# Projection of a fused convolution and gated FFN: from 128x32 to 64x64 TensorE tiles

## The chip, the cores and the metric

The kernel runs on one core of a Trainium2 chip. The metric is the time of one execution in device microseconds (us); several executions are made and their median is given. Besides the times there is one profiled execution, in which a hardware profiler records every instruction of the engines: TensorE (PE, with its weight loads as PEld), VectorE (DVE), ScalarE (ACT), GpSimd (POOL), SyncE (SP), and the DMA queues that SP, ACT and POOL feed.

## The reference

Two steps follow each other. First a causal lightweight convolution over the sequence: each of 8 heads (24 of 192 channels each) has 7 taps, made positive by a softmax. Then a gated FFN on each of 32768 tokens, from 192 channels to 1536 and back:

```
x: (8, 4096, 192)   weight: (8, 7)
w = softmax(weight, axis=-1)
out = einsum('hk,bskhg->bshg', w, x_unf)      # 7 shifted copies of x
gate = maximum(x @ w_gate, 0.0)               # 192 -> 1536
val = x @ w_val                               # 192 -> 1536
return gate * val @ w_out                     # 1536 -> 192
```

The result is float32, 32768 x 192. The kernel computes its matmuls in float16 with float32 accumulation in PSUM.

## The kernel before

The work is cut into 16 units. A unit holds 1024 consecutive tokens of two batch rows ("streams", `st`), so 2048 tokens, in two windows `w` of 512. The convolved input of a unit, `xc`, has 64 channels of stream 0 on partitions 0 to 63 and the same channels of stream 1 on partitions 64 to 127, in three chunks `c`.

*Gates* (`gate_val`). For each window and each of 12 slices `f` of 128 hidden channels, six matmul pairs are made: three chunks for the gate and three for the value. A pair is two row tiles of 64x128, one per stream, each streaming 512 columns (line 530). ACT applies the relu from PSUM into `gr` (line 539), DVE multiplies it with the value into `hT` (line 540). All PSUM tiles named `ps` (128 x 2 banks x 512) come from one ring of four buffers, in the order of allocation; a slice `f` takes two, so two slices are in flight.

*Projection* (`project_columns`, line 550). After both windows, `hT` (128 hidden channels of one `f` on the partitions) is multiplied with `Wo`. The 192 output channels are cut into three tiles `p` of 64, and these into two banks `b` of 32. A slot consists of four matmuls of 128 rows x 32 columns side by side, one for each pair of window and stream; 12 slots accumulate over `f`. That makes 72 slots, 288 matmuls, per unit. DVE turns each tile by 32x32 blocks into the output buffer `out_s` (`turn_out`, line 564), and `store` sends the unit to DRAM in four DMAs on SP's queue, each from 32 partitions in rows of 192 channels, 768 bytes (line 572). `out_s` has two buffers.

*Convolution of later units.* Units 2 to 15 are convolved by DVE, ACT and POOL beside the matmuls. For unit `u+2`, in unit `u`: POOL copies the loaded `x_e` into `x_p` (line 436), SP transposes it by eight DMA transposes into `x_r` (line 438). During the projection ACT makes the first tap of a part on DVE's account (`lane_first`, line 484) and then 13 products of the other part (line 464), and DVE makes 13 lane steps (lines 495 and 505). `TAPS` and `STEPS` say after which projection tile which products and steps are issued. In the next unit POOL adds the products up (line 473). Each engine works through its instructions in order, and so does SP's queue.

*Start.* Unit 0 and unit 1 are convolved on TensorE with band matrices: `conv(2)` and `conv(3)` make the second part of unit 1 by eight matmuls each (line 353), five ACT copies (line 366) and five DMA transposes (line 385). `conv(3)` stands behind the first projection tile of unit 0. The last unit uses another projection (`project`, line 586) with `Wo` as the moving operand.

What sets the order is the program itself: the schedule is written out by hand, the framework adds the semaphores.

Of the kernel before, what the change touches and what calls it, by code (L numbers as in the profile page):

```python
# [8 lines left out]
FP = mybir.dt.float32  # L9
F16 = mybir.dt.float16  # L10
# [5 lines left out]
def kernel(  # L16
# [12 lines left out]
    nc = tc.nc  # L29

    B, S, D = x.shape
# [4 lines left out]
    NB = B // 2  # L36
    NCH = D // 64
    NBLK = D // 32
    NFF = DFF // 128
    WIN = 512  # L40
    NWIN = S // WIN
    SUB = 112
    STEPS = [4, 5, 4]
    TAPS = [(6, 5, 4), (3, 2), (1, 0)]
    GSUB = 5
    WARM = [2, 3, 1]
    STEPS0 = [1, 0, 2, 3, 4]
# [6 lines left out]
    FLAT = NCH * UNIT  # L54
    LDVE = 1280
# [6 lines left out]
    const = ctx.enter_context(tc.tile_pool(name="const", bufs=1))  # L62
    epool = ctx.enter_context(tc.tile_pool(name="epool", bufs=1))
    rpool = ctx.enter_context(tc.tile_pool(name="rpool", bufs=2))
    apool = ctx.enter_context(tc.tile_pool(name="apool", bufs=1))
# [4 lines left out]
    psum = ctx.enter_context(tc.tile_pool(name="psum", bufs=4, space=bass.MemoryType.PSUM))  # L70
# [5 lines left out]
    def staged(i, j):  # L76
        return stages[i][:, XH * j : XH * (j + 1)]

    def load_x(g, streams=range(2)):


        bp, toks = GROUPS[g]
        xt = staged(g // 3, g % 3).rearrange("p (j s d) -> p j s d", s=2, d=D)
        for st in streams:
            b = bp + NB * st
            last = toks[-1] == S - SUB or toks[-1] - toks[-2] != SUB
            n_full = len(toks) - int(last)
            lo = toks[0] - PAD
            src = bass.AP(
                tensor=x.tensor,  # L90
                offset=x.offset + (b * S + lo) * D,
                ap=[[D, 128], [SUB * D, n_full], [1, D]],
            )
            nc.gpsimd.dma_start(out=xt[:, 0:n_full, st, :], in_=src)
            if last:
                nc.gpsimd.dma_start(
                    out=xt[0 : SUB + PAD, len(toks) - 1, st, :],
                    in_=x[b, toks[-1] - PAD : toks[-1] + SUB, :],
                )
        return xt  # L100
# [61 lines left out]
    with nc.allow_low_precision("one of the terms is not zero"):  # L162
        nc.vector.tensor_reduce(
            out=Z[:, 112 : 112 + HR],
            in_=eye[:].rearrange("p (g i) -> p i g", i=HR),
# [4 lines left out]
        out=mask[:, :, 0],  # L170
        in_=eye[:].rearrange("p (g i) -> p g i", i=HR),
# [17 lines left out]
    for half in range(2):  # L189
        nc.tensor.matmul(  # L190
            out=raised[half][:, 0, 0 : SUB * H // 2],
            lhsT=zeros[:, 0:128],
            rhs=zeros[:, 0 : SUB * H // 2],
            start=True,
            stop=False,
# [2 lines left out]

    Wg = const.tile([128, NCH, DFF], F16)
    Wv = const.tile([128, NCH, DFF], F16)  # L200
    Wo = const.tile([128, NFF, D], F16)
    CUTS = [0, 128, 256, 512, 896, DFF]
    HALVES = [0, 128, 256, 512, 896, 1280, DFF]

# [16 lines left out]
    for s in range(5):  # L221
# [8 lines left out]
        out=mx[:], in_=spread[:, 0, 0:KW], axis=mybir.AxisListType.X, op=ALU.max, negate=True  # L230
# [8 lines left out]
        out=prod[:],  # L239
# [11 lines left out]
        out=blocks[:],  # L251
# [11 lines left out]
    for half, copy in enumerate((nc.vector.tensor_copy, nc.scalar.copy)):  # L263
        for j in range(128 // HR):
# [3 lines left out]
                out=raised[half][:, 0, 0 : SUB * H // 2].rearrange("p (h t) -> p h t", t=SUB)[  # L268
                    :, :, s0 + lo : s0 + hi
                ],  # L270
                lhsT=Z[:, 112 - HR * j : 240 - HR * j],
                rhs=blocks[:, H // 2 * half : H // 2 * (half + 1), lo:hi],
                start=False,
                stop=(j == 128 // HR - 1),
# [3 lines left out]
            out=bands[half][:].rearrange("p h t -> p (h t)"), in_=raised[half][:, 0, 0 : SUB * H // 2]  # L278
# [7 lines left out]
    for c in range(NCH):  # L286
        r0 = 0
        while r0 < 64:
# [3 lines left out]
            for st in range(2):  # L292
                nc.sync.dma_start(
                    out=tap[64 * st + r0 : 64 * st + r1, c, :],
# [158 lines left out]
    def shifted(u, c, k, t, n):  # L453
        o = HALO - KW + 1 + k + t
        return xrs[u][:, c, o : o + n]
# [4 lines left out]
    def product(u, k):  # L460
        prods[u, k] = apool.tile([128, FLAT - LDVE], FP, name=f"prod{k}")
        for at, n, c, t in pieces(LDVE, FLAT):
            if k or t == 0:
                nc.scalar.activation(  # L464
                    out=prods[u, k][:, at - LDVE : at - LDVE + n],
                    in_=shifted(u, c, k, t, n),
                    func=ACTF.Copy,
                    scale=tap[:, c, k : k + 1],
                )
# [70 lines left out]
            nc.vector.tensor_tensor(out=h[:, f], in0=gr[:], in1=pss[1][:], op=ALU.mult)  # L540
        return h

    def project_columns(hs, p):


        ps = psum.tile([128, 2, 512], FP, name="ps")
        for b in range(2):
            for f in range(NFF):
                for s in range(4):
                    nc.tensor.matmul(  # L550
                        out=ps[32 * s : 32 * s + 32, b, :],
                        lhsT=Wo[:, f, 64 * p + 32 * b : 64 * p + 32 * b + 32],
                        rhs=hs[s // 2][:, f, s % 2, :],
                        start=(f == 0),
                        stop=(f == NFF - 1),
                        tile_position=(0, 32 * s),
                        skip_group_check=True,
                    )
        return ps

    def turn_out(ps, o, p):


        nc.vector.transpose(  # L564
            out=o[:, :, 64 * p : 64 * p + 64].rearrange("p t (b c) -> p b t c", b=2),
            in_=ps[:].rearrange("p b (t c) -> p b t c", c=32),
        )

    def store(o, bp, w0):
        for s in range(4):  # L570
            row0 = (bp + NB * (s % 2)) * S + WIN * (w0 + s // 2)
            nc.sync.dma_start(
                out=out[row0 : row0 + WIN, :].rearrange("(t p) d -> p t d", p=32),
                in_=o[32 * s : 32 * s + 32],
            )

    def project(bp, w, h, st, final, o):


        parts = [range(4)] if not final else [range(2), range(2, 3), range(3, 4)]  # L580
        row0 = (bp + NB * st) * S + WIN * w
        for n, qs in enumerate(parts):
            ps = psum.tile([128, 2, 512], FP, name="ps")
            for i, q in enumerate(qs):
                for f in range(NFF):
                    nc.tensor.matmul(  # L586
                        out=ps[:, i // 2, D * (i % 2) : D * (i % 2) + D],
                        lhsT=h[:, f, st, 128 * q : 128 * (q + 1)],
                        rhs=Wo[:, f, :],
                        start=(f == 0),  # L590
                        stop=(f == NFF - 1),
                    )
            os_ = o[:, qs[0] : qs[0] + len(qs), :].rearrange("p (a b) d -> p a (b d)", a=(len(qs) + 1) // 2)
            k = len(qs)
            a, m = (k + 1) // 2, min(k, 2) * D
            copy = nc.vector.tensor_copy if n == 1 else nc.scalar.copy
            copy(out=os_, in_=ps[:, 0:a, 0:m])  # L597
            (nc.scalar if n == 2 else nc.sync).dma_start(
                out=out[row0 + 128 * qs[0] : row0 + 128 * (qs[0] + k), :].rearrange(
                    "(q p) d -> p q d", p=128  # L600
                ),
                in_=o[:, qs[0] : qs[0] + k, :],
            )
# [12 lines left out]
    both_halves(nc.vector.tensor_copy, 1, Wv)  # L616
    lane_load(2)
    xts[2] = load_x(2)
    nc.gpsimd.dma_start(out=Wo[:], in_=moe_w_out.rearrange("(c p) d -> p c d", p=128))
    for u in range(NUNIT):  # L620
        lane = 1 <= u < NUNIT - 1
        if lane:
            add(u + 1, 1)
        if u == 1:
            lane_load(3)
            add(2, 2)
            add(2, 3)
        if u + 2 < NUNIT:
            lane_turn(u + 2)
        if u == 0:  # L630
            xts[3] = load_x(3)
        if 0 < u < NUNIT - 3:
            lane_load(u + 3)
        if lane:
            for k in range(4 if u == 1 else 2, KW - 1):
                add(u + 1, k)
        hs = [gate_val(u, w) for w in range(2)]
        if lane:
            add(u + 1, KW - 1)
        if u == 0:  # L640
            xc[1] = xcpool.tile([128, NCH, UNIT], F16, name="xc")
            conv(2)
        del xc[u]
        bp, w0 = u * UNIT // S, u * UNIT % S // WIN
        lane = None
        if u + 2 < NUNIT:
            lane_first(u + 2)
            lane = lane_rest(u + 2)
        o = opool.tile([128, UNIT // 64, D], FP, name="out_s")
        if u == NUNIT - 1:  # L650
            for i in range(4):
                project(bp, w0 + i // 2, hs[i // 2], i % 2, i == 3, o[:, 4 * i : 4 * i + 4, :])
            continue
        for p in range(3):
            ps = project_columns(hs, p)
            if lane:
                for k in TAPS[p]:
                    product(u + 2, k)
                for _ in range(STEPS[p]):
                    next(lane)  # L660
            turn_out(ps, o, p)
            if u == 0 and p == 0:
                conv(3)
        store(o, bp, w0)


# [28 lines left out]
```

## Time and profile before

| what | value |
|---|---|
| median of 3 runs | 768.77 us (767.99 to 769.97) |
| profiled execution | 768.63 us |
| its span | 766.9 us |
| TensorE busy | 761.4 us, 99% |
| DVE busy | 670.9 us, 87% |
| ACT busy | 598.6 us, 78% |
| POOL busy | 422.9 us, 55% |
| granted TensorE clock | 0.999 of full |
| chain by line | 530: 64.9%, 550: 30.6%, 586: 2.1% |

The profiled execution takes 1.7 us more than its span, which runs from the first to the last instruction. In a group of instructions, "busy, mean ns" is the total busy time and the duration of one; matmul durations overlap, so their pace is read from starts and from the chain, not from the mean. "idle before" is the time that the engine stood still ahead of these instructions, with what ended it. The chain of work that ended last is followed back from the end: what stands on it sets the time.

### The profile page before, as it was taken

To read this page: it belongs to the slowest core of one execution; us is meant where nothing else is said; L and a number is where in the kernel's file an instruction comes from. 1 tells how busy PE (TensorE), PEld (TensorE's weight loads), DVE (VectorE), ACT (ScalarE), POOL (GpSimd) and SP (SyncE) were. 2 spreads that over 40 slices of the span, in tenths; PEclk is the share of its full clock that TensorE was granted. 3 is DMA by queue.
4 is the path that set the end of the run, shared out by engine and by line. 5 is a ranking of instruction groups with operands and counts; after the bars stand their busy time and mean duration, and the time that the engine had idled before them with its cause. 6 is when DMAs were issued, how large, how long until landed. Compare 5 with 4: busy or idle time off the path is not lost.

```text
span 766.9 us, 21548 instructions
## 1 busy us (share of the span) xinstructions
PE 761.4 (99%) x9402; PEld 378.6 (49%) x9402; DVE 670.9 (87%) x630; ACT 598.6 (78%) x622; POOL 422.9 (55%) x190
## 2 busy tenths in 40 slices
PE   8999999999999999999999999999999999999998
PEld 5554444444444444444444444444444444444448
DVE  6888999989899998989989899898998989896690
ACT  6798887978778787787978879788797877874471
POOL 9407749095591946829277391864909558191000
PEclk9999999999999999999999999999999999999999
DMA  9927829092390905609065190832909142040402
GB/s 143 152 51 130 92 58 111 3 136 31 78 90 3 150 17 93 74 15 152 2 107 61 36 131 3 127 40 60 107 3 138 29 82 45 2 84 2 83 2 83
DMA packets 123214, 53.79 MB, mean 70 GB/s; under 512 B 87648, under 2 KB 123120, under 8 KB 123120
## 3 DMA queue, kind: packets, MB, share of 16 engines
q1 hardware_dynamic: 86192, 38.06, 31.5%
q0 software_dynamic: 36768, 14.26, 18.3%
q8 instruction: 73, 1.20, 0.7%
q14 instruction: 21, 0.17, 0.1%
q10 hardware_dynamic: 160, 0.10, 0.0%
HBM read 29.40 MB, written 25.17 MB: 71 GB/s over the span
## 4 chain that ended last, share of the span: by engine, by line
PE 99%; ACT 0%; POOL 0%; DVE 0%; issue 0%; POOLq 0%
PE ps L530 65%; PE ps L550 31%; PE ps L586 2%; PE ps L330 0%; PE ps L353 0%; PE ps L180 0%; DVE hT L540 0%; ACT gr L539 0%; PE ps L267 0%; PE ps L190 0%; ACT xc L341 0%; PE ps L186 0%; POOL prod L160 0%; POOL rows L144 0%; ACT out_s L597 0%
## 5 line engine op out<-in xcount | busy, mean ns | idle before, releaser
L539 ACT ACTIVATE gr<-ps 128x1024 f16<-128x1024 f32 x384 | 393.2, 1024 | 146.4 <-PE ps L530 146.1
L540 DVE TENSOR_TENSOR hT<-gr,ps 128x1024 f16<-128x1024 f16 x384 | 468.9, 1221 | 38.5 <-ACT gr L539 12.0
L473 POOL TENSOR_TENSOR prod<-prod,prod 128x1792 f32<-128x1792 f32 x70 | 278.6, 3980 | 257.6 <-DVE prod L505 212.4
L530 PE MATMUL ps<-xc,Wg 64*128 64x512 f16 x2304 | 312.1, 376 | 0.6 <-ACT xc L341 0.6
L530 PE MATMUL ps<-xc,Wv 64*128 64x512 f16 x2304 | 311.9, 376 | 0.2 <-DVE hT L540 0.2
L550 PE MATMUL ps<-hT,Wo 128*32 128x512 f16 x4320 | 236.0, 379 | 0.0
L530 PEld LDWEIGHTS <-Wv 64*128 64x128 f16 x2304 | 129.9, 94 | 119.0 <-issue 0.5
L530 PEld LDWEIGHTS <-Wg 64*128 64x128 f16 x2304 | 111.2, 94 | 138.8 <-issue 6.9
L550 PEld LDWEIGHTS <-Wo 128*32 128x32 f16 x4320 | 114.1, 97 | 120.3 <-issue 6.3
L464 ACT ACTIVATE prod<-x_r,tap 128x1024 f32<-128x1024 f16 (+1 forms) x182 | 172.9, 1043 | 0.1
L495 DVE SCALAR_TENSOR_TENSOR acc<-x_r,tap,acc 128x1024 f32<-128x1024 f16 (+1 forms) x140 | 114.2, 873 | 2.4 <-ACT acc L484 2.4
L564 DVE STREAM_TRANSPOSE out_s<-ps 128x1024 f32<-128x1024 f32 x45 | 56.1, 1247 | 33.2 <-PE ps L550 33.1
L473 POOL TENSOR_TENSOR xc<-prod,prod 128x1792 f16<-128x1792 f32 x14 | 55.7, 3976 | 1.1
L436 POOL COPY x_p<-x_e 128x1536 f16<-128x1536 f16 x28 | 40.3, 1468 | 2.1 <-DMA x_e<-in_x_dram 2.1
L399 POOL DMA_DIRECT2D x_e<-in_x_dram x28 | 25.1, 900 | 4.2 <-POOL x_p L436 4.2
L495 DVE SCALAR_TENSOR_TENSOR xc<-x_r,tap,acc 128x1024 f16<-128x1024 f16 (+1 forms) x28 | 23.4, 878 | 0.0
L484 ACT ACTIVATE acc<-x_r,tap 128x1024 f32<-128x1024 f16 (+1 forms) x28 | 21.6, 823 | 0.5 <-DMA x_r<-x_p 0.5
L586 PE MATMUL ps<-Wo,hT 128*128 128x192 f16 x192 | 16.0, 246 | 0.0
L586 PEld LDWEIGHTS <-hT 128*128 128x128 f16 x192 | 15.8, 98 | 0.4 <-issue 0.4
L597 ACT COPY out_s<-ps 128x768 f32<-128x768 f32 (+2 forms) x5 | 3.2, 639 | 12.7 <-PE ps L586 12.7
L597 DVE COPY out_s<-ps 128x192 f32<-128x192 f32 x1 | 0.4, 358 | 13.3 <-PE ps L586 13.3
L505 DVE TENSOR_SCALAR prod<-x_r,tap 128x768 f32<-128x768 f16 x14 | 8.6, 612 | 0.0
(55 smaller groups left out, 62.8 us busy)
## 6 DMA issues: line engine op xcount, KB each, us to landing
out_dram<-out_s SPq DMA_DIRECT2D x63, 384.0 KB
x_e<-in_x_dram POOLq DMA_DIRECT2D x28, 384.0 KB, 10.2
x_r<-x_p SPq DMA_TRANSPOSE x112
out_s<-in_x_dram POOLq DMA_DIRECT2D x4, 240.0 KB, 6.8
prod<-in_x_dram SPq DMA_DIRECT2D x3, 192.0 KB
Wo<-in_moe_w_out_dram POOLq DMA_DIRECT2D x1, 576.0 KB, 10.5
out_s<-in_x_dram POOLq DMA_DIRECT2D x2, 192.0 KB, 4.7
Wg<-in_moe_w_gate_dram POOLq DMA_DIRECT2D x1, 240.0 KB, 6.1
```

What stands on the lines that cost most here:

```text
L399: nc.gpsimd.dma_start(out=xe[:, :, st, :, :].rearrange("p j c r -> p j (c r)"), in_=bass.AP(tensor=x.tensor, offset=x.offset + row * D, ap ...
L436: nc.gpsimd.tensor_copy(out=xp[:, :, :, st, :], in_=xe[:, :, st, :, :])
L464: nc.scalar.activation(out=prods[u, k][:, at - LDVE : at - LDVE + n], in_=shifted(u, c, k, t, n), func=ACTF.Copy, scale=tap[:, c, k : k + 1],)
L473: nc.gpsimd.tensor_tensor(out=p0[:] if k < KW - 1 else flat(u)[:, LDVE:FLAT], in0=p0[:], in1=prods.pop((u, k))[:], op=ALU.add,)
L484: nc.scalar.activation(out=accs[u][:, at : at + n], in_=shifted(u, c, 0, t, n), func=ACTF.Copy, scale=tap[:, c, 0:1],)
L495: nc.vector.scalar_tensor_tensor(out=(flat(u) if k == KW - 1 else acc)[:, at : at + n], in0=shifted(u, c, k, t, n), scalar=tap[:, c, k : k ...
L530: nc.tensor.matmul(out=pss[i][:, st, :], lhsT=W[64 * st : 64 * st + 64, c, 128 * f : 128 * (f + 1)], rhs=xcb[64 * st : 64 * st + 64, c, WI ...
L539: nc.scalar.activation(out=gr[:], in_=pss[0][:], func=ACTF.Relu)
L540: nc.vector.tensor_tensor(out=h[:, f], in0=gr[:], in1=pss[1][:], op=ALU.mult)
L550: nc.tensor.matmul(out=ps[32 * s : 32 * s + 32, b, :], lhsT=Wo[:, f, 64 * p + 32 * b : 64 * p + 32 * b + 32], rhs=hs[s // 2][:, f, s % 2, ...
L564: nc.vector.transpose(out=o[:, :, 64 * p : 64 * p + 64].rearrange("p t (b c) -> p b t c", b=2), in_=ps[:].rearrange("p b (t c) -> p b t c" ...
L586: nc.tensor.matmul(out=ps[:, i // 2, D * (i % 2) : D * (i % 2) + D], lhsT=h[:, f, st, 128 * q : 128 * (q + 1)], rhs=Wo[:, f, :], start=(f ...
```

## The change

Each projection slot now consists of four 64x64 tiles: two halves `r` of the 128 hidden channels by two streams `st`, and all 64 output channels of a tile `p` at once. A half `r` of the rows writes one bank (window `b`), the other half the other bank; so in one turn each bank gets only half of the sum. A second turn of 12 slots swaps the halves and completes both. Matmuls, slots and streamed columns per unit are the same in number.

Between the two turns of a tile ACT copies one column of each bank out (`between_turns`), and the second turn's matmuls wait for it. The six turns of the three tiles are interleaved: (0,0), (1,0), (0,1), (2,0), (1,1), (2,1), as (tile, turn). Products are issued after first turns and lane steps before the transpose after second turns, with new `STEPS` and `TAPS`; `conv(3)` stands behind turn (2,0).

`Wo` is laid out anew, so that a tile `p` holds channels 32p to 32p+31 and 96+32p to 96+32p+31. It is loaded into the buffer `prod0` and regrouped by two POOL copies in unit 0. The partitions of `out_s` now stand for stream and half row, so the store has eight DMAs, each of rows of 96 channels, 384 bytes.

```diff
-    STEPS = [4, 5, 4]
-    TAPS = [(6, 5, 4), (3, 2), (1, 0)]
+    STEPS = [6, 5, 2]
+    TAPS = [(6, 5), (4, 3), (2, 1, 0)]
...
-    def project_columns(hs, p):
-        ps = psum.tile([128, 2, 512], FP, name="ps")
-        for b in range(2):
-            for f in range(NFF):
-                for s in range(4):
+    def project_turn(hs, p, ps, turn):
+        for f in range(NFF):
+            for r in range(2):
+                b = (r + turn) % 2
+                for st in range(2):
                     nc.tensor.matmul(
-                        out=ps[32 * s : 32 * s + 32, b, :],
-                        lhsT=Wo[:, f, 64 * p + 32 * b : 64 * p + 32 * b + 32],
-                        rhs=hs[s // 2][:, f, s % 2, :],
-                        start=(f == 0),
-                        stop=(f == NFF - 1),
-                        tile_position=(0, 32 * s),
+                        out=ps[64 * st : 64 * st + 64, b, :],
+                        lhsT=Wo[64 * r : 64 * r + 64, f, p, :],
+                        rhs=hs[b][64 * r : 64 * r + 64, f, st, :],
+                        start=(turn == 0 and f == 0),
+                        stop=(turn == 1 and f == NFF - 1),
+                        tile_position=(64 * r, 64 * st),
                         skip_group_check=True,
                     )
-        return ps
+
+    def between_turns(ps):
+        nc.scalar.copy(out=turned_by[:], in_=ps[:, :, 0])
...
-            out=o[:, :, 64 * p : 64 * p + 64].rearrange("p t (b c) -> p b t c", b=2),
+            out=o[:].rearrange("p t (b d) -> p b t d", b=2)[:, :, :, 32 * p : 32 * p + 32],
...
-        for s in range(4):
-            row0 = (bp + NB * (s % 2)) * S + WIN * (w0 + s // 2)
-            nc.sync.dma_start(
-                out=out[row0 : row0 + WIN, :].rearrange("(t p) d -> p t d", p=32),
-                in_=o[32 * s : 32 * s + 32],
-            )
+        for q in range(4):
+            row0 = (bp + NB * (q // 2)) * S + WIN * w0
+            for b in range(2):
+                nc.sync.dma_start(
+                    out=out[
+                        row0 + WIN * b : row0 + WIN * (b + 1), D // 2 * (q % 2) : D // 2 * (q % 2 + 1)
+                    ].rearrange("(t p) d -> p t d", p=32),
+                    in_=o[32 * q : 32 * q + 32, :, D // 2 * b : D // 2 * (b + 1)],
+                )
...
-    nc.gpsimd.dma_start(out=Wo[:], in_=moe_w_out.rearrange("(c p) d -> p c d", p=128))
+    loaded = apool.tile([128, FLAT - LDVE], FP, name="prod0")
+    plain = loaded[:].bitcast(F16)[:, 0 : NFF * D]
+    nc.gpsimd.dma_start(
+        out=plain.rearrange("p (c d) -> p c d", d=D), in_=moe_w_out.rearrange("(c p) d -> p c d", p=128)
+    )
...
+            wide = plain.rearrange("k (f a p d) -> k f a p d", a=2, p=3, d=32)
+            for a in range(2):
+                nc.gpsimd.tensor_copy(out=Wo[:, :, :, 32 * a : 32 * a + 32], in_=wide[:, :, a, :, :])
...
-        for p in range(3):
-            ps = project_columns(hs, p)
-            if lane:
-                for k in TAPS[p]:
-                    product(u + 2, k)
-                for _ in range(STEPS[p]):
-                    next(lane)
-            turn_out(ps, o, p)
-            if u == 0 and p == 0:
-                conv(3)
+        tiles = [None] * 3
+        for p, turn in ((0, 0), (1, 0), (0, 1), (2, 0), (1, 1), (2, 1)):
+            if turn == 0:
+                tiles[p] = psum.tile([128, 2, 512], FP, name="ps")
+            project_turn(hs, p, tiles[p], turn)
+            if turn == 0:
+                between_turns(tiles[p])
+                if lane:
+                    for k in TAPS[p]:
+                        product(u + 2, k)
+                if u == 0 and p == 2:
+                    conv(3)
+                continue
+            if lane:
+                for _ in range(STEPS[p]):
+                    next(lane)
+            turn_out(tiles[p], o, p)
         store(o, bp, w0)
```

More of the change, by code (lines that the diff above doesn't have):

```diff
@@ L200 @@
     Wv = const.tile([128, NCH, DFF], F16)
-    Wo = const.tile([128, NFF, D], F16)
+    Wo = const.tile([128, NFF, 3, 64], F16)
     CUTS = [0, 128, 256, 512, 896, DFF]
@@ L541, in gate_val @@
         return h
-    def project_columns(hs, p):
-        ps = psum.tile([128, 2, 512], FP, name="ps")
-        for b in range(2):
-            for f in range(NFF):
-                for s in range(4):
-                    nc.tensor.matmul(
-                        out=ps[32 * s : 32 * s + 32, b, :],
-                        lhsT=Wo[:, f, 64 * p + 32 * b : 64 * p + 32 * b + 32],
-                        rhs=hs[s // 2][:, f, s % 2, :],
-                        start=(f == 0),
-                        stop=(f == NFF - 1),
-                        tile_position=(0, 32 * s),
+    def project_turn(hs, p, ps, turn):
[3 more added lines that the diff above has]
+                for st in range(2):
+                    nc.tensor.matmul(
+                        out=ps[64 * st : 64 * st + 64, b, :],
[4 more added lines that the diff above has]
+                        tile_position=(64 * r, 64 * st),
                         skip_group_check=True,
                     )
-        return ps
+    turned_by = const.tile([128, 2], FP)
+    def between_turns(ps):
+        nc.scalar.copy(out=turned_by[:], in_=ps[:, :, 0])
     def turn_out(ps, o, p):
         nc.vector.transpose(
-            out=o[:, :, 64 * p : 64 * p + 64].rearrange("p t (b c) -> p b t c", b=2),
+            out=o[:].rearrange("p t (b d) -> p b t d", b=2)[:, :, :, 32 * p : 32 * p + 32],
             in_=ps[:].rearrange("p b (t c) -> p b t c", c=32),
@@ L588, in project @@
                         lhsT=h[:, f, st, 128 * q : 128 * (q + 1)],
-                        rhs=Wo[:, f, :],
+                        rhs=Wo[:, f, :, :].rearrange("k p (a d) -> k a p d", a=2),
                         start=(f == 0),
```

## The prediction

> **What bounds the kernel now.** I read busy shares first, then the chain in order of time, then the end of one projection engine by engine, then the DMA queue of SyncE. The page and the chain of work that ended last:
>
> ```profile
> PE 761.4 (99%) x9402; PEld 378.6 (49%) x9402; DVE 670.9 (87%) x630; ACT 598.6 (78%) x622; POOL 422.9 (55%) x190
> L550 PE MATMUL ps<-hT,Wo 128*32 128x512 f16 x4320 | 236.0, 379 | 0.0
> L484 ACT ACTIVATE acc<-x_r,tap 128x1024 f32<-128x1024 f16 (+1 forms) x28 | 21.6, 823 | 0.5 <-DMA x_r<-x_p 0.5
> ...
> 107.42 31.19 PE ps L530 x288
> 138.60 15.65 PE ps L550 x288
> 154.26 31.19 PE ps L530 x288
> ```
>
> TensorE never stops: each unit costs 31.19 + 15.65 = 46.84 us of it. 31.19 us over 144 row-tiled pairs is 216.6 ns a pair; 15.65 us over 72 groups of four is 217.4 ns, and inside the projection a group starts 215.7 ns after the one before. Both stream 512 columns per slot, so only the array's pace, its switches between tile shapes, and new waits can move the time. Now one projection (it starts at 138.53) on ACT, DVE, POOL and PE, in the timeline:
>
> ```profile
> 137.79 0.81 PE L530 MATMUL ps<-xc,Wv 64*128 64x512 f16 x6
> 138.53 0.83 PE L550 MATMUL ps<-hT,Wo 128*32 128x512 f16 x12
> ...
> 138.92 1.54 ACT L484 ACTIVATE acc<-x_r,tap 128x1024 f32<-128x1024 f16 x2
> 140.36 12.33 ACT L464 ACTIVATE prod<-x_r,tap 128x768 f32<-128x768 f16 x13
> 155.05 1.02 ACT L539 ACTIVATE gr<-ps 128x1024 f16<-128x1024 f32 x1 [2.36 <-PE ps L530]
> ...
> 140.19 3.27 DVE L495 SCALAR_TENSOR_TENSOR acc<-x_r,tap,acc 128x1024 f32<-128x1024 f16 x4
> 143.95 1.25 DVE L564 STREAM_TRANSPOSE out_s<-ps 128x1024 f32<-128x1024 f32 x1 [0.49 <-PE ps L550]
> 154.31 1.25 DVE L564 STREAM_TRANSPOSE out_s<-ps 128x1024 f32<-128x1024 f32 x1 [1.11 <-PE ps L550]
> ...
> 153.35 3.99 POOL L473 TENSOR_TENSOR prod<-prod,prod 128x1792 f32<-128x1792 f32 x1 [17.44 <-DVE prod L505]
> ```
>
> ACT has 2.36 us to spare per projection; DVE waits for TensorE before its last transpose. And SyncE's queue, then DMA share and rate in two windows (last two columns):
>
> ```profile
> 45.51 18.39 SPq L385 DMA_TRANSPOSE xc<-out_s  x10
> 64.00 4.96 SPq L572 DMA_DIRECT2D out_dram<-out_s  x4
> 80.10 11.22 SPq L438 DMA_TRANSPOSE x_r<-x_p  x8
> 92.65 1.55 ACT L484 ACTIVATE acc<-x_r,tap 128x1024 f32<-128x1024 f16 x2 [0.47 <-DMA x_r<-x_p]
> ...
> 155.59 4.55 SPq L572 DMA_DIRECT2D out_dram<-out_s  x4
> 160.34 15.38 SPq L438 DMA_TRANSPOSE x_r<-x_p  x8
> ...
> 156.50:160.50 4.00, 4.00 (x42) 1.94 (x38) 3.78 (x4) 3.19 (x4) 3.82 (x4) 1.00 0.98 183
> 757.00:759.00 2.00, 2.00 (x27) 2.00 (x25) 0.00 (x0) 0.00 (x0) 0.00 (x0) 1.00 0.62 197
> ```
>
> Stores and the x_r transposes share one queue in order. In steady state x_r has landed some 9 us before ACT's L484 asks for it (transposes over at 175.7, L484 at 185.8). In unit 1 it is already late: ACT waited 0.47 us at 92.65. In the windows a store of 768-byte packets from 32 partitions runs at 183 GB/s / (0.98 x 16) = 11.7 GB/s an engine, 66 ns a packet; the last stores, from 128 partitions, at 197 / (0.62 x 16) = 19.9, 39 ns.
>
> **The change, part by part.**
>
> *Matmuls.* 288 per unit before and after, in 72 slots of four 512-column streams. A gain in pace is excluded: every row streams about 2.37 columns a ns. The nearest rows are the groups of four (215.7 ns) and the pairs whose two halves are row tiles, as the new ones are (216.6 ns). I take the second: 0.9 ns x 72 x 15 = **+1.0 us** (ends 0 and 1.0). Weight loads double to 64 columns. A run of 40 conv matmuls (L330), half of them with 32-column loads, takes 0.57 us of the chain, so such a load costs at most 14 ns; four of 64 columns, at most 114 ns, lie under a 216 ns slot as long as they overlap it.
>
> *Switches of tile shape.* L530 to L550 costs 0.09 us over the usual step (137.79 to 138.53 is 0.74, six matmuls being 0.65), back 0.10. Whether 64x128 to 64x64 is a switch no row shows. I keep it: 0; without it, 30 x 0.095 = -2.8 us. [...]
>
> *Fences on ACT.* Each first turn is followed by a 128x2 copy on ACT (rows for tiny operations: 0.20 and 0.27 us; I take 0.27), and the second turn of that tile waits for it. Turns last 12 x 215.7 = 2.59 us; an end reaches another engine 0.24 us later (143.95 - 138.53 - 5.18). Counted from the projection's start: L484 ends at 1.93; fence 0 waits for 2.83, done 3.10, needed at 5.18; four products of 0.948 us (12.33 / 13) to 6.89; fence 1 done 7.16, needed 10.35; four more; fence 2 done 11.2, needed 12.94; five products to 16.0. The next gate's first relu (L539) is due at 155.05 - 138.53 = 16.52. So TensorE waits nowhere: 0, covered by ACT's 2.36 us idle, of which 0.5 us is left. Queued behind each fence are the products and then that relu; once the 0.5 us is gone, TensorE stops for the rest, since the third gate group needs the first one's buffers.
>
> *DVE.* Six lane steps from 1.66 end at 6.6; transpose 0 waits for turn 3 (7.77 + 0.24) and ends at 9.2; five steps to 13.5, transpose 1 to 14.7, two short steps to 15.7, transpose 2 at 15.78, as before (154.31 - 138.53). 0.
>
> *GpSimd.* Its first add starts when the last products end, at 16.0 instead of 14.8: x_p 1.2 us later, behind the store in SP's queue anyway; 0. The two Wo copies of unit 0 (128x1152; L436 copies 1536 in 1.47 us) fall into an idle stretch from 32 to 61 us, 9 us ahead of the projection that needs them: 0.
>
> *Half rows, steady state.* Eight stores, 4096 packets of 384 bytes, in place of four with 2048. By bytes a packet costs half of 64 ns, 32; by packets 64; x_e's 384-byte load packets take 51 (DMA records). I take 45. The store then flows 256 x 45 = 11.5 us an engine instead of 16, at most 16.4: x_r lands 3 to 8 us later, inside its 9. 0; the cover ends near 77 ns a packet.
>
> *The start: conv(3) and unit 1.* conv(3) moves behind turn (2,0), its five ACT moves (2.0 us) behind all products, to 60.1 to 62.1. Its PSUM pair now comes after the three tiles, so the second gate group of unit 1 (61.15) needs the buffer of transpose 2, free at 61.9: **+0.75 us**. Its DMA transposes go from 62.1; the fifth waits for the fourth's landing, as before (4.5 us), so SP reaches the store at about 71.7 instead of 64.0. Eight issues, two free and six at the flow's 1.44 us, plus some 2 us against the x_e load: SP is free at 83.3 instead of 80.1. Eight transposes of x_r (11.2 us) and 1.3 us to be seen: 95.8 instead of 92.65. L484 then ends at 97.35, fence 0 at 97.6, just when TensorE needs it (92.44 + 5.18), but ACT's products end at 110.6 against a relu due at 108.96: **+1.6 us**. Ends: at 32 ns SP is free at 80 and this is 0; at 64 ns x_r comes at 99.3, fence 0 holds TensorE 3.5 us and the relu is 1.6 us late: 5.1.
>
> Sum: 1.0 + 0.75 + 1.6 = 3.35 on the profiled 768.63 (span 766.9 + 1.7): 772.0, with the median 0.14 above it 772.1. 0.3% (2.3 us) is about what can be told from no change.
>
> **Rivals.**
>
> A. The shape change is none, because the row halves stay: 0.095 us x 30 gone. 768.77 + 3.35 - 2.8 = 769.3, and with the two upper terms at their low ends (0 and 0) 768.77 + 0.75 - 2.8 = 766.7: not slower. It decides (under the 2.3 us) once a switch falls by 0.035 us, and gives a gain only with the upper terms low. For it: the change keeps two row halves throughout. Against: nothing in the trace switches columns alone at full clock.
>
> B. Half rows hold x_r back in every unit. Past 77 ns a packet each ns is 0.256 us a unit on ACT's products and the next relu: at 84 ns 1.8 us x 12 units + 8 at the start, 798. For it: 66 against 39 ns shows that these stores already suffer from their source. Against: bytes per packet halve. [...]
>
> C. Quarters don't overlap as halves do: loads of 64 columns laid bare cost up to 114 x 1080 = 123 us (892). Against: 97 ns loads are hidden at L550 and L530 alike.
>
> D. ACT falls behind in every unit: fences that cost 0.5 us each rather than 0.27, or a late wake-up, use 0.7 us and more of its 0.5: with 1 us in all too much, 14 units give 786. For it: only 0.5 us is left; against: the 0.27 us row.
>
> **How the numbers follow.** Forecast 0.45, A 0.25, B 0.10, C 0.07, D 0.13. The forecast's own range is 769.5 to 776 (terms 0.75 to 6.9); A reaches down to 766.5; D and most of B lie under 792; left out are C, the worst of B and a little below. Faster: half of A, 0.12. Within 0.3%: the other half and the forecast's low part, 0.30. Slower: the rest, 0.58.
>
> **What would show it.** Steady projections on the chain of 15.65 to 15.75 us, gates 31.19; more says C, less than 15.6 says A. A gap of TensorE before unit 1's first gates and another about 108 to 112 us; none elsewhere. ACT's wait for x_r once in unit 1, not later; if in each, B. ACT's relu waiting 0.5 us instead of 2.36 after each projection; if it waits for nothing and TensorE does, D. Store packets near 45 ns. I am wrong if TensorE idles over 0.1 us in a steady unit.

## The result and the profile after

The changed kernel takes 769.9 us in the median of 12 executions, the one before 768.42 us in the same row: a ratio of 1.0019, 95% interval 1.0011 to 1.0026. Two more rows, told below, give 1.0008 (0.9999 to 1.0017) and 1.0010 (1.0001 to 1.0019). So its median is 0.1 to 0.2% higher in all three rows, 0.6 to 1.5 us where 3.35 were forecast, and in one row the interval still touches no change. It also spreads more: 768.9 to 771.93 us.

Two lines of the page of the changed kernel, busy shares and the new projection's matmuls:

```profile
PE 761.2 (99%) x9402; PEld 392.1 (51%) x9402; DVE 670.4 (87%) x630; ACT 603.8 (79%) x667; POOL 424.8 (55%) x192
...
L550 PE MATMUL ps<-hT,Wo 64*64 64x512 f16 x4320 | 236.2, 376 | 0.0
```

TensorE is as full as before. The chain in order of time (start, duration, what) says where the little that was lost lies:

```profile
60.51 31.32 PE ps L530 x288
91.84 15.66 PE ps L550 x288
107.50 31.30 PE ps L530 x288
138.80 15.66 PE ps L550 x288
154.46 31.19 PE ps L530 x288
185.65 15.66 PE ps L550 x288
```

From unit 3 on a unit takes 31.19 + 15.66 = 46.85 us, against 46.84. Units 1 and 2 have gates of 31.32 and 31.30. From there on the units of the two kernels agree to 0.01 us. ACT at unit 1's projection, in the changed kernel's timeline:

```profile
94.62 1.55 ACT L484 ACTIVATE acc<-x_r,tap 128x1024 f32<-128x1024 f16 x2 [2.38 <-DMA x_r<-x_p]
96.08 0.13 ACT L563 COPY turned_by<-ps 128x2 f32<-128x2 f32 x1
96.12 3.84 ACT L464 ACTIVATE prod<-x_r,tap 128x768 f32<-128x768 f16 x4
...
103.69 4.88 ACT L464 ACTIVATE prod<-x_r,tap 128x768 f32<-128x768 f16 x5
108.47 2.14 ACT L539 ACTIVATE gr<-ps 128x1024 f16<-128x1024 f32 x2
```

The wait for x_r has grown from 0.47 to 2.38 us, and at 108.47 two relus stand back to back: ACT came late to unit 2. DVE came late too, since its lane steps wait for L484. Its last transpose of unit 1, and the group of unit 2 that needs the buffer of this transpose:

```profile
108.15 1.25 DVE L568 STREAM_TRANSPOSE out_s<-ps 128x1024 f32<-128x1024 f32 x1
109.45 0.82 PE L530 MATMUL ps<-xc,Wv 64*128 64x512 f16 x6
```

The transpose ends at 109.40 and the group starts at 109.45, 0.06 us later than its turn. A steady unit's ACT, for comparison:

```profile
141.56 0.16 ACT L563 COPY turned_by<-ps 128x2 f32<-128x2 f32 x1 [0.92 <-PE ps L550]
...
155.26 1.02 ACT L539 ACTIVATE gr<-ps 128x1024 f16<-128x1024 f32 x1 [0.93 <-PE ps L530]
```

Here ACT still has 0.93 us to spare before the first relu. SP's queue in the changed kernel, up to unit 2:

```profile
45.42 27.41 SPq L385 DMA_TRANSPOSE xc<-out_s  x10
72.93 7.31 SPq L577 DMA_DIRECT2D out_dram<-out_s  x8
80.33 13.01 SPq L438 DMA_TRANSPOSE x_r<-x_p  x8
```

conv(3)'s transposes hold SP until 72.8 us, the first store comes after them, and the x_r transposes for unit 3 after that, until 93.3 instead of 91.3. They start only 0.2 us later than before (80.33 against 80.10). The rest is their run, 13.0 us instead of 11.2: in the DMA records the store's packets move until 87.8 us, beside them, where before they had ended at 77.7.

### The profile page after: what moved, and what is told of

Read it like the earlier page. It is cut to its first block, busy times and chain, and to the rows that moved or that the text cites. A ratio compares the mean times of both kernels' runs of the same rounds, so it can differ in the third digit from the quotient of the medians.

```text
span 767.0 us, 21736 instructions
## 1 busy us (share of the span) xinstructions
PE 761.2 (99%) x9402; PEld 392.1 (51%) x9402; DVE 670.4 (87%) x630; ACT 603.8 (79%) x667; POOL 424.8 (55%) x192
## 4 chain that ended last, share of the span: by engine, by line
PE 99%; ACT 0%; DMA 0%; DVE 0%; issue 0%
PE ps L530 65%; PE ps L550 31%; PE ps L593 2%; PE ps L330 0%; PE ps L353 0%; DMA w<-in_weight_dram 0%; PE ps L180 0%; DVE hT L540 0%; PE ps L267 0%; ACT gr L539 0%; PE ps L190 0%; ACT xc L341 0%; PE ps L186 0%; ACT out_s L604 0%
## 5 line engine op out<-in xcount | busy, mean ns | idle before, releaser
L540 DVE TENSOR_TENSOR hT<-gr,ps 128x1024 f16<-128x1024 f16 x384 | 468.7, 1221 | 36.9 <-ACT gr L539 10.2
L530 PE MATMUL ps<-xc,Wg 64*128 64x512 f16 x2304 | 312.8, 376 | 0.6 <-ACT xc L341 0.6
L530 PE MATMUL ps<-xc,Wv 64*128 64x512 f16 x2304 | 312.7, 376 | 0.2 <-DVE hT L540 0.2
L550 PE MATMUL ps<-hT,Wo 64*64 64x512 f16 x4320 | 236.2, 376 | 0.0
L530 PEld LDWEIGHTS <-Wv 64*128 64x128 f16 x2304 | 131.0, 94 | 118.3 <-issue 0.6
L530 PEld LDWEIGHTS <-Wg 64*128 64x128 f16 x2304 | 113.5, 94 | 136.4 <-issue 6.7
L550 PEld LDWEIGHTS <-Wo 64*64 64x64 f16 x4320 | 124.9, 107 | 109.9 <-issue 6.3
L464 ACT ACTIVATE prod<-x_r,tap 128x1024 f32<-128x1024 f16 (+1 forms) x182 | 175.0, 1043 | 0.0
L563 ACT COPY turned_by<-ps 128x2 f32<-128x2 f32 x45 | 7.0, 155 | 22.6 <-PE ps L550 20.8
L484 ACT ACTIVATE acc<-x_r,tap 128x1024 f32<-128x1024 f16 (+1 forms) x28 | 21.6, 821 | 2.4 <-DMA x_r<-x_p 2.4
```

The source lines that it names most:

```text
L464: nc.scalar.activation(out=prods[u, k][:, at - LDVE : at - LDVE + n], in_=shifted(u, c, k, t, n), func=ACTF.Copy, scale=tap[:, c, k : k + 1],)
L484: nc.scalar.activation(out=accs[u][:, at : at + n], in_=shifted(u, c, 0, t, n), func=ACTF.Copy, scale=tap[:, c, 0:1],)
L530: nc.tensor.matmul(out=pss[i][:, st, :], lhsT=W[64 * st : 64 * st + 64, c, 128 * f : 128 * (f + 1)], rhs=xcb[64 * st : 64 * st + 64, c, WI ...
L550: nc.tensor.matmul(out=ps[64 * st : 64 * st + 64, b, :], lhsT=Wo[64 * r : 64 * r + 64, f, p, :], rhs=hs[b][64 * r : 64 * r + 64, f, st, :] ...
```

## The experiments

Two theories stood against each other. S, the start: the whole loss lies in units 0 to 2, by way of conv(3)'s late place, the late first store and a late x_r, and it varies with the landing of that x_r. W, the whole run: the new projection or its stores cost something in every unit. A third, H, joined later: long executions are long in the head, before the first projection.

**The first store behind the transposes.** The changed kernel; only the order on SP differs, once:

```diff
             lane_turn(u + 2)
+        if u == 1:
+            store(*unit0)
...
-        store(o, bp, w0)
+        if u == 0:
+            unit0 = o, bp, w0
+        else:
+            store(o, bp, w0)
```

> The changed kernel with the store of unit 0 issued after the eight transposes of x_r for unit 3, so that SP is free for them as soon as x_p is copied (80.3 us). Theory S: ACT's wait for x_r in unit 1 falls from 2.4 us to 0.5 us or less, the gaps of 0.05 us at 109 and 110 us go, the one at 61 us (0.12) stays; median 768.7 to 769.1 (ratio 1.000 to 1.001) and a spread as narrow as that of before. Theory W: the median stays at 769.5 to 770.5 although the wait is gone.

Beside it ran the changed kernel itself:

> The changed kernel once more, in one row with the others, and a second trace of it. In its first trace it lost 0.27 us against the profiled execution of before (0.13 us ahead of unit 1's second gate group, 0.12 us early in unit 2), while its median was 1.5 us up with a spread of 3 us. Theory S (start): the rest of the loss is also at the start, where x_r of unit 3 lands at a different time in each execution: this trace, if it is a longer one, shows steady units of 46.85 us all the same and longer gaps in units 1 and 2. Theory W (whole run): steady units differ, each a little longer than 46.85 us. Time by both: 769.5 to 770.5, ratio about 1.002.

Measured: the changed kernel 769.05 us, 1.0008 (0.9999 to 1.0017); with the first store behind, 768.75 us, 0.9998 (0.9989 to 1.0007). The timeline of ACT in the second:

```profile
92.25 1.53 ACT L484 ACTIVATE acc<-x_r,tap 128x1024 f32<-128x1024 f16 x2
...
108.41 1.02 ACT L539 ACTIVATE gr<-ps 128x1024 f16<-128x1024 f32 x1 [0.93 <-PE ps L530]
```

The wait for x_r is gone and unit 2 begins like every other unit. Unit 1 keeps its gap at 61 us and has another of 0.11 us at 76 us, where the last of conv(3)'s late transposes lands (76.09) just after TensorE wanted it; in the first trace it had landed at 73.93. The steady units are 46.85 us too, so what W would name is still in it, and the kernel is as fast as before within the interval. The trace of the changed kernel in this row shows something that S did not hold: an execution of 769.73 us whose ACT wait was only 1.5 us and whose unit 2 lost nothing. Its delay lies at 22 us:

```profile
20.75 0.23 PE L330 MATMUL ps<-band,out_s 118*32 118x112 f16 x2
22.15 0.63 PE L330 MATMUL ps<-band,out_s 118*32 118x112 f16 x38 [1.17 <-DMA out_s<-in_x_dram]
```

A load of x for conv(1) arrived late. The change does not touch that load. That made theory H, and the pair was run again.

> The changed kernel a third time, beside the next one on the same chip, for the spread: in the run before, 6 of 11 executions of it were above 769.0 us, none of 11 with the first store behind the transposes, 5 of 33 of the kernel before. Theory S: again about half above 769, the longer executions because x_r of unit 3 lands later. Theory H (head): the long executions differ in the first 25 us, where loads of x arrive late (the second trace had a wait of 1.2 us for one at 22 us); then the two kernels of this pair have the same share of long executions.

> The changed kernel with the first store behind the x_r transposes, a second time. Theory S: at most 1 or 2 of 11 above 769.0, median 768.5 to 768.9. Theory H: as many long executions as the changed kernel beside it.

Measured: the changed kernel 769.23 us, 1.0010 (1.0001 to 1.0019), 8 of 11 executions above 769.0; with the first store behind 768.68 us, 1.0002 (0.9994 to 1.0011), 2 of 11. Over both rows it is 14 of 22 against 2 of 22, and 7 of 60 for the kernel before. H alone would give the pair equal shares: it explains single executions, not the difference.

**conv(3) ahead.** In the changed kernel conv(3) follows conv(2), before the projection:

```diff
             conv(2)
+            conv(3)
...
-                if u == 0 and p == 2:
-                    conv(3)
```

> The changed kernel with conv(3) right behind conv(2), ahead of the first projection. Theory S: its ACT moves end about 47.5 us instead of 61, the first store starts when transpose 2 is done (62.0), x_r for unit 3 is as early as before (ACT waits 0.5 us or less), and the gaps at 61 and 109 us go; a new gap of about 0.7 us opens at 44.7 us, where the first projection tile needs a buffer of conv(2) until its moves end at 45.4. Median 768.9 to 769.5, narrow spread. Theory W: 769.5 to 770.5 plus that gap.

Measured: 768.71 us, 1.0005 (0.9996 to 1.0013). SP's queue in the timeline:

```profile
45.31 16.56 SPq L385 DMA_TRANSPOSE xc<-out_s  x10
62.03 7.31 SPq L577 DMA_DIRECT2D out_dram<-out_s  x8
79.28 11.41 SPq L438 DMA_TRANSPOSE x_r<-x_p  x8
```

The first store starts at 62.03 and the transposes at 79.28, no later than before (64.00 and 80.10). TensorE at conv(3)'s new place:

```profile
44.39 0.57 PE L353 MATMUL ps<-out_s,band 118*112 118x240 f16 x4 [0.32 <-DVE hT L540]
```

ACT no longer waits for x_r and the gaps of units 1 and 2 are gone, as S said. The new gap came where I had not put it: inside conv(3), which waits for DVE's last multiply, not before the projection tile. It is 0.48 us from start to start (582 ns where 102 is the step).

**Half rows alone.** The kernel before, each of its four stores cut in two:

```diff
-                out=out[row0 : row0 + WIN, :].rearrange("(t p) d -> p t d", p=32),
-                in_=o[32 * s : 32 * s + 32],
+                out=out[row0 : row0 + WIN, D // 2 * b : D // 2 * (b + 1)].rearrange("(t p) d -> p t d", p=32),
+                in_=o[32 * s : 32 * s + 32, :, D // 2 * b : D // 2 * (b + 1)],
```

> The kernel before with nothing but its stores cut into half rows (eight DMAs of 384-byte packets per unit in place of four of 768). Theory S: unit 0's store is done on SP at about 71.3 us, ahead of the x_p copy (80.1), so nothing moves: ratio 0.9995 to 1.0005. Theory W, in the form that half rows cost something in every unit: ratio 1.001 to 1.002. Packets of 32 ns in both.

Measured: 768.38 us, 0.9999 (0.9990 to 1.0007). Its SP queue ends the first store at 61.70 + 7.46 = 69.2 us, ahead of the transposes at 77.97. Half rows cost nothing in themselves.

**conv(3) late, alone.** The kernel before, with its old projection and full rows:

```diff
-            if u == 0 and p == 0:
+            if u == 0 and p == 2:
                 conv(3)
```

> The kernel before with nothing but conv(3) moved behind the third projection tile (full rows, 128x32 tiles, no fences). Theory S (the start makes the loss): a gap of 0.1 to 1 us ahead of unit 1's second gate group, the first store reaches SP about 72 us instead of 64, x_r of unit 3 is seen about 2 us late; without fences TensorE does not wait for ACT's late L484, so beyond the gap nothing: ratio 1.0002 to 1.0015. Theory W (loss in every unit of the new projection): ratio 0.9995 to 1.0005, since no unit has the new projection.

Measured: 769.37 us, 1.0011 (1.0003 to 1.0020): a loss like that of the changed kernel, without any of its new matmuls, fences or half rows. TensorE in its timeline:

```profile
62.85 0.82 PE L530 MATMUL ps<-xc,Wg 64*128 64x512 f16 x6
64.11 0.82 PE L530 MATMUL ps<-xc,Wv 64*128 64x512 f16 x6 [0.43 <-DVE hT L540]
```

And ACT, one projection later:

```profile
95.37 1.55 ACT L484 ACTIVATE acc<-x_r,tap 128x1024 f32<-128x1024 f16 x2 [2.82 <-DMA x_r<-x_p]
...
109.06 1.91 ACT L539 ACTIVATE gr<-ps 128x1024 f16<-128x1024 f32 x2
```

The last transpose of DVE there, and the group of unit 2 behind it:

```profile
108.90 1.25 DVE L564 STREAM_TRANSPOSE out_s<-ps 128x1024 f32<-128x1024 f32 x1
110.20 0.82 PE L530 MATMUL ps<-xc,Wv 64*128 64x512 f16 x6 [0.36 <-DVE out_s L564]
```

The gap before the group at 64.11 (1.26 us after 62.85, where 0.65 is the step) comes from conv(3)'s moves, which push ACT's relus. conv(3) stands behind the whole projection here and its moves end at 61.9 us, not at 61.2 as in the changed kernel, so unit 1 loses more, 0.69 us against 0.14. Unit 2 then loses 0.54 us through the same wait for x_r. My expectation that nothing follows without fences was wrong: DVE's lane steps wait for L484 as well, and with them the last transpose comes late, whose buffer TensorE needs, fence or not.

**How much a late x_r costs.** Unit 0's store issued twice, whole and by a quarter (two of its eight DMAs), in the changed kernel:

```diff
         store(o, bp, w0)
+        if u == 0:
+            store(o, bp, w0)                # e9: store(o, bp, w0, range(1))
```

> The changed kernel with the store of unit 0 issued twice, so that SP and the DMA queue are held some 8 us longer ahead of the x_r transposes for unit 3. It measures what a late x_r costs. Theory S: x_r is seen about 8 us later (102.5 instead of 94.6), L484 ends at 104, fence 0 comes at 104.2 where TensorE wanted it at 97.0, so TensorE waits 7 us at the third turn of unit 1, and ACT's late products add up to 1.5 us at the start of unit 2: 776 to 779. Theory W, or a cover that I overlooked: no wait at the third turn, 769 to 770.5.

> The changed kernel with a quarter of unit 0's store (two of its eight DMAs) issued twice: a small delay of x_r for unit 3, to see from where it costs. So far ACT's wait of 1.5 us for x_r cost TensorE nothing, 2.4 us cost 0.09, 2.7 us cost 0.43, 13.4 us cost 10.2 at the fence and 2.5 at half clock. Theory S, with a cover of 2.3 us and one for one beyond it: some 2.5 to 3 us more of waiting, 5 us in all, and TensorE standing 2.5 to 3 us, at the starts of unit 2's first groups or at the third turn: ratio 1.003 to 1.005, 771 to 772.5. If the cover is larger: under 770.

Measured: 781.63 us, 1.0163 (1.0148 to 1.0178), and 775.57 us, 1.0077 (1.0053 to 1.0100). Both delays came out larger than I had meant, 13.41 and 7.80 us of waiting: 16 issues hold SP for 18.68 us where eight held it for 7.31, and why the second copies are slower was not found. TensorE's timeline in the first of the two:

```profile
91.84 5.37 PE L550 MATMUL ps<-hT,Wo 64*64 64x512 f16 x96
107.38 13.46 PE L550 MATMUL ps<-hT,Wo 64*64 64x512 f16 x192 [10.16 <-ACT turned_by L563]
```

Windows of the same (the last three columns: granted clock, DMA share, GB/s):

```profile
107.00:110.00 3.00, 2.62 (x28) 1.44 (x31) 3.00 (x4) 3.00 (x6) 0.00 (x0) 0.50 0.00 0
110.00:113.00 3.00, 3.00 (x36) 1.62 (x32) 1.97 (x4) 3.00 (x6) 0.00 (x0) 0.50 0.00 0
113.00:116.00 3.00, 3.00 (x60) 1.84 (x56) 3.00 (x4) 2.09 (x4) 0.00 (x0) 0.95 0.00 0
```

The fence is the path: the third turn waits 10.16 us for ACT's copy, which stands behind L484. After it TensorE gets half its clock for 5.9 us, which costs 2.9 us more by the starts of the slots (the expectation of the quarter run says 2.5).

**Two more traces**, each of a further execution of the changed kernel:

> The changed kernel, one look, for a trace of another execution. Theory S: its time above that of the steady units is the sum of the head's delay and of the gaps in units 1 and 2, and these grow with ACT's wait for x_r beyond 2.3 us. Theory W: a remainder that neither holds.

> As the look before: another execution of the changed kernel, with the same two theories.

They took 768.92 and 769.55 us. All traces of the changed kernel, as excess over the trace of before (first projection matmul 43.78 us, unit 1 and 2 gates 31.18 us, last relevant instruction, ACT's final copy, at 763.51):

```
trace      ACT's wait   head    unit 1   unit 2   15 projections   sum    final copy
first        2.38      -0.08     0.14     0.12        0.15         0.33     0.32
second       1.5       +0.81     0.14     0.00        0.15         1.10     1.10
third        2.71      -0.06     0.14     0.46        0.15         0.69     0.69
fourth       2.8       -0.22     0.14     0.51        0.15         0.58     0.58
fifth        3.01      -0.11     0.14     0.76        0.15         0.94     0.93
```

The four terms leave no remainder, so nothing else in these executions is longer; W is left with 15 times 0.01 us. Unit 2's loss follows ACT's wait one for one beyond 2.3 us: 2.38 gives 0.12, 2.71 gives 0.46, 3.01 gives 0.76. The fifth trace's ACT, with two relus back to back at its end:

```profile
95.23 1.55 ACT L484 ACTIVATE acc<-x_r,tap 128x1024 f32<-128x1024 f16 x2 [3.01 <-DMA x_r<-x_p]
...
109.07 1.92 ACT L539 ACTIVATE gr<-ps 128x1024 f16<-128x1024 f32 x2
```

And the third trace's last transpose on DVE, and TensorE, where a value group of unit 2 starts 1.06 us after the one before, 0.65 being the step:

```profile
108.52 1.25 DVE L568 STREAM_TRANSPOSE out_s<-ps 128x1024 f32<-128x1024 f32 x1
...
108.76 0.81 PE L530 MATMUL ps<-xc,Wg 64*128 64x512 f16 x6
109.82 0.82 PE L530 MATMUL ps<-xc,Wv 64*128 64x512 f16 x6 [0.24 <-DVE out_s L568]
```

TensorE stops for DVE's last transpose here, not for a relu: in all four traces of the changed kernel in which unit 2 loses time, and with conv(3) late alone, this group starts 0.04 to 0.06 us after that transpose ends, and its wait is on DVE. The relu is close behind. In the third trace the first relu of unit 2 ends at 109.85 and the multiply behind it starts at 109.88, which costs another 0.04 us two groups on; by itself it would have cost some 0.45 us (an estimate from these starts). So the late L484 reaches TensorE on two paths that end almost together.

## Why the prediction was right or wrong

The direction and the place held: the loss lies in units 1 and 2 and comes from conv(3)'s late place. The size did not, and the last link was another. Three terms of the sum failed. Unit 1's +1.6 us was 0 to 0.76, and it followed the late x_r to ACT's products and relu alone, where TensorE stopped first for DVE's transpose, which had been put at 0. The matmuls' +1.0 was 0.15. The ring's +0.75 was 0.13, by another cause. That the first row's median, 769.9, lies within the forecast's range of 769.5 to 776 is partly luck: the later medians, 769.05 and 769.23, lie below it. Step by step:

- **Matmuls, +1.0 us.** A projection is 15.66 us against 15.65 on the chain, 0.01 us each or 0.15 in all. The 216.6 ns of the row-tiled pairs are 31.19 us over 144, an average that holds the switch between the shapes; from start to start the pairs step by 215 or 216 ns in the trace of before (142 of 143 steps), as the groups of four do. The step failed by setting an average beside a step: both rows have the same pace, and the new quarters keep it (215 or 216 ns). The 0.01 us is the first slot, 240 ns long instead of 227.
- **Switches, 0.** Right: L530 to L550 is 306 ns from matmul to matmul in both kernels, back 312 before and 308 after, so 64x128 to 64x64 takes as long as 64x128 to 128x32. That it would was the author's assumption: no row of before has the new pair of shapes. Rival A, with no switch, is out.
- **Weight loads.** Hidden, as argued: loads of 64 columns are 107 ns long instead of 97, and the slots behind the first keep their steps of 215 or 216 ns. Rival C is out.
- **Fences on ACT, 0 with 0.5 us left.** Right in kind, wrong in price: a fence moves the next product by 0.04 to 0.06 us (96.08 to 96.12, 141.56 to 141.62), not by 0.27. So ACT has 0.93 us left in steady units. Rival D is out. An isolated small instruction was the wrong row for one that stands in a stream: the copy at 96.08 is 0.13 us long, and the next product starts 0.04 us after its start.
- **Half rows, steady state, 0.** Right, and by more than I took: 384-byte packets average 31.6 ns in the DMA records, the low end of my range, and the core's DMA moves 170 GB/s at a share of 0.90, against 183 at 0.98 in the same window (156.5 to 160.5 us). In every steady unit x_r keeps 8 us or more. Rival B is out.
- **Ring of PSUM buffers, +0.75 us.** 0.12 to 0.14 measured, and by another cause. I took the ring to go round by allocation, as the description of the kernel says. In the trace the second gate group of unit 1 waits on ACT, not on DVE: it starts at 61.23, when conv(3)'s last move has ended at 61.18, and not at transpose 2's end, 61.9. That fits buffers handed out in the order of their release.
- **Unit 1, +1.6 us.** The experiments show the chain up to L484: late conv(3), late store, late x_r, late L484. From there I followed only ACT's products to the next relu. TensorE stopped first for the other branch, late lane steps and a late last transpose on DVE; the relu's branch ends within 0.1 us of it. The size is 0 to 0.76 us in five traces. With packets at 32 ns SP was free at 80.2 us, not 83.3; the transposes then took 13.0 us instead of the 11.2 that I took from before, which my end of 0 at 32 ns left out; x_r was seen between 94.6 and 95.2, not at 95.8; and the late L484 is covered up to 2.3 us of waiting.

The terms with their measured sizes give 0.15 + 0.13 + 0 to 0.76 = 0.3 to 1.0 us, which agrees with the two later rows (0.60 and 0.64 us in the medians). The 1.5 us of the first row, with executions up to 771.9, is not explained in full: no trace of an execution of the changed kernel above 769.73 was taken. A later x_r would do it, since the slope is known, and moving the first store removes nearly all executions above 769.0; but that its longest ones come from there is argued, not shown.

## What to carry to other kernels

TensorE was 99% busy and the new work streams as many columns as the old: the steady unit moved by 0.02% here (46.84 to 46.85 us), and what was left to predict was the start, where queues still carry set-up work. List what each queue holds ahead of the first unit's data. When an input comes late, follow it into every engine that reads it, not only into the one that waits for it first. Compare a step with a step: an average over a stage holds its switches too (here 217.4 ns against 215 or 216). Price a small instruction added to a stream by its effect on the next start (here 0.04 to 0.06 us), not by its length when it stands alone (0.27). A load that has no slack before a change (here 0.47 us late already) can turn a reordering on its queue into time, and into spread.

## What the hardware showed that was not expected

- In two runs a stop of TensorE cost more than its length. After 10.2 us of waiting at a fence, with unit 0's store issued twice, the slots took 427 ns from start to start instead of 216 for 5.9 us, at a granted clock of 0.50; after 4.55 us in the quarter experiment they did for 2.9 us, with a mean clock of 0.66 from 103 to 107 us. Added cost: 2.9 and 1.4 us. The clock fell 2.4 and 4.1 us after the last matmul. What lowers the clock and what raises it again is not shown. One of the four executions of the quarter experiment kept a clock of 1.00 and took 772.03 us, the others 775.5 to 775.7. A gap of 1.17 us left the clock at 1.00 (the second trace of the changed kernel).
- Store packets from 32 partitions took 31.6 ns for 384 bytes after and 62 for 768 before in the DMA records, in proportion to their bytes, while those of 768 bytes from 128 partitions took 39 (the last stores).
